# First row tile of weights and tokens loaded in row halves on two DMA queues, all its high parts on ScalarE, in a gated mix of attention and MLP

## Chip, cores and metric

The kernel runs on one core of one Trainium2 chip. The metric is the device time of one execution in microseconds. The kernel before takes 392.97 us (median of 3 runs, 392.96 to 393.01).

## The reference

For tokens x (2048 rows of 448), two branches are mixed by a gate g, one number per row:

```python
g = sigmoid((x * gate_w).sum(-1))          # 2048
qkv = x @ wqkv                             # 448 -> 3 * 448, 16 heads of 28
# each row attends to 8 rows: itself and those 2, 4, .. 14 before it
a = (softmax(q . k * scale) @ v) @ wo      # 448 -> 448
b = relu(x @ w1 + b1) ** 2 @ w2 + b2       # 448 -> 1792 -> 448
out = g * a + (1 - g) * b
```

All arrays are float32.

## The kernel before, in words

Each matmul operand is split into a high part (rounded to the matmul's reduced type, fp32r) and a low part (what is left of it), and a product is made of three matmuls: high by high, high by low and low by high. High parts are mostly made by ScalarE (an ACTIVATE that copies), low parts by VectorE (a subtraction, which needs the high part).

The contraction over 448 is cut into row tiles of 128, 128, 128 and 64. The tokens are taken in four chunks of 512 columns (x is transposed on the host). For each chunk q, k and v are made (function `qkv_first` for the first chunk, `qkv_two` for the others), stored to DRAM and read back by the attention, which GpSimd and VectorE work on while TensorE makes the MLP branch. The output projection by wo comes last. Most instructions of ScalarE, VectorE, GpSimd and of SP's DMA queue are ordered by a planner in the kernel (`Plan`): each job has a cost, its dependencies and a priority, and TensorE's own time is advanced by constants (`MM448`, `MM512`, `START` for the first real matmul, `FIRST` for the three row tiles of the first chunk). The planner decides the order in which instructions are built into each engine's queue; no time of it is waited for on the chip.

The start of the program is written out by hand (lines 801 to 843) and runs ahead of the planner:

- lines 806 and 807: WARM = 19 matmuls of zeros (128 by 128 against 256 columns) on TensorE;
- lines 809 to 813: the buffers `raws[0]` (first weight block, wq, with two columns for the gate: 450 columns) and `rx` (first chunk of tokens, 512 columns), each with four row tiles. ScalarE's queue loads row tile 0 of the tokens, 128 rows, in two halves of 256 columns;
- lines 814 to 821: SP's queue loads row tile 0 of the weights (128 rows, 225 KB), then row tiles 1 to 3 of weights and tokens in turn, and after these the weights of k and v;
- lines 830 to 839: the split. For row tile 0, ScalarE makes the weights' high part (`wqh`, line 831), VectorE the high part of the first half of the tokens' columns (line 836), VectorE the low part of the weights (`wql`, line 838) and of the first half (line 839); ScalarE then makes the second half's high part (line 834) and VectorE its low part. For the later row tiles ScalarE makes both high parts;
- `qkv_first`, line 429: q of the first chunk, for the row tiles 0 to 2 with 12 matmuls each, 36 in all. A matmul holds 128 tokens (a slice of x) as its stationary operand and streams 452 columns of weights (450 and a gap). For row tile 0 the order is: high by high for the first and second 128 tokens, then those two by the low weights, then the low tokens by the high weights, and the same for the third and fourth 128 tokens (which need the second half of the token columns).

After this come the 64-row tiles and k and v (line 341), and so on to the last projection (line 1154), the last mix (line 1037) and the last store. Near the end, ScalarE copies the attention outputs read back (tiles named ot) into SBUF and PSUM (lines 1110, 1115, 1120, 1121), VectorE subtracts (1122, 1124), and tiny ACTIVATEs (line 736, "touches") mark points of TensorE's order for the dependency tracking.

Of the kernel before, what the change touches and what calls it, by code (L numbers as in the profile page):

```python
# [9 lines left out]
AF = mybir.ActivationFunctionType  # L10
# [4 lines left out]
P = 128  # L15
# [7 lines left out]
CH = 512  # L23
NQ = D + 2
# [7 lines left out]
MM448, MM512 = 189.2, 216.0  # L32
PE_LAT = 175.0
LAT = 60.0
START = 4900.0
ORDER = (3, 0, 1, 2)
WARM = 19
FIRST = (2700.0, 2350.0, 2300.0)
PP_BUFS = 4
ST_BUFS = 3  # L40
BT_BUFS = 8
# [142 lines left out]
def gated_mix_kernel(ctx: ExitStack, tc: tile.TileContext, xT, wqkv, w1, w2, wo, b1, b2, out):  # L184
    nc = tc.nc

    def f32(ap):
        return ap.bitcast(F32)

    def woven(w):  # L190

        if w.shape[1] == NQ:
            return bass.AP(tensor=w.tensor, offset=w.offset, ap=[list(w.ap)[0], [1, NH], [D // 2, 2]])
        return w.rearrange("p (i n) -> p n i", i=2)

    def woven_out(pt, n):
        return (pt[:, :2 * NH] if n == NQ else pt[:, :n]).rearrange("p (n i) -> p n i", i=2)
# [85 lines left out]
    def x_tiles(c):  # L283
        if c % 2:
            x_place[0] = xpool.tile([P, 8 * CH + 16], F32R, tag="x", name=f"x{c}")
            return [x_slot(j, 0 if c == 1 else 16) for j in range(4)]
        return [xap.tile([P, 2, CH], F32R, tag=f"x{j}", name=f"x{c}_{j}") for j in range(4)]
# [11 lines left out]
    wqh = ap.tile([P, 3, NP + 2 * D], F32R, name="wqh")  # L299
    wql = ap.tile([P, 3, NP + 2 * D], F32R, name="wql")  # L300
# [119 lines left out]
    def qkv_first(x):  # L420
        four = range(4)
        q = accs(0, 0, four, "bbbb")
        for k in range(3):
            todo = [full(x, q[i], i, 0, (k,)) for i in four]
            for some in ((0, 1), (2, 3)) if k == 0 else (four,):
                for j in range(3):
                    for i in some:
                        acc, a, w, *_ = todo[i][j]
                        nc.tensor.matmul(woven_out(acc.pt, NQ), a, woven(w), start=k == j == 0, stop=False)  # L429
            plan.pe(FIRST[k])  # L430
        for acc in q:
# [373 lines left out]

    for _ in range(WARM):
        nc.tensor.matmul(warm[:, :2 * P].rearrange("p (i n) -> p i n", i=2), zero, zeros, start=True, stop=True)  # L807

    raws = [rawp.tile([P, 4, 512], F32, tag="raw", name="wqraw0")]
    rx = rawp.tile([P, 4, 512], F32, tag="raw", name="xraw0")  # L810
    halves = slice(0, 256), slice(256, CH)
    for cols in halves:
        nc.scalar.dma_start(rx[:, 0, cols], xT[0, :, 0, cols])
    for k in range(4):
        if k < 3:
            nc.sync.dma_start(raws[0][:, k, :NQ], wqkv[0, :, k])
        else:
            for b, rows in ((0, slice(0, 64)), (1, slice(64, P))):
                nc.sync.dma_start(raws[0][rows, k, :NQ], wqkv[b, rows, k])
        if k:  # L820
            nc.sync.dma_start(rx[:, k], xT[0, :, k])
# [7 lines left out]
    x = X(x_tiles(0))  # L829
    for k in range(3):  # L830
        nc.scalar.activation(wqh[:, k, :NQ], raws[0][:, k, :NQ], AF.Copy)
        for n, cols in enumerate(halves if k == 0 else (slice(0, CH),)):
            if k or n:
                nc.scalar.activation(x.h[k][:, cols], rx[:, k, cols], AF.Copy)
            else:
                nc.vector.tensor_copy(x.h[k][:, cols], rx[:, k, cols])
            if not n:
                nc.vector.tensor_sub(wql[:, k, :NQ], raws[0][:, k, :NQ], f32(wqh[:, k, :NQ]))
            nc.vector.tensor_sub(x.l[k][:, cols], rx[:, k, cols], f32(x.h[k][:, cols]))
    nc.scalar.activation(w7h[:, :NQ], raws[0][:, 3, :NQ], AF.Copy)  # L840
    nc.vector.tensor_sub(w7l[:, :NQ], raws[0][:, 3, :NQ], f32(w7h[:, :NQ]))
# [3 lines left out]

    plan.t, plan.wire = START, 15000.0
    plan.now = 9800.0
# [64 lines left out]
    for c in range(4):  # L912
        x = xs[c]
# [305 lines left out]
    rows = wo_d.rearrange("(i b) n -> i b n", b=14)  # L1219
# [31 lines left out]
    for g in range(2, 2 * NF):  # L1251
# [5 lines left out]
        if not f:  # L1257
            x, slots = X([nxt[j][0] for j in range(4)]), [nxt[j][1] for j in range(4)]
# [105 lines left out]
```

## Time and profile before

| what | value |
| --- | --- |
| median of 3 runs | 392.97 us (392.96 to 393.01) |
| the profiled execution's own time | 392.84 us |
| its span | 391.1 us |
| TensorE busy | 386.5 us (99%), 3829 matmuls |
| VectorE, ScalarE, GpSimd busy | 260.3, 205.4, 260.6 us |
| DMA | 73.75 MB, mean 189 GB/s |

The profiled execution's own time stands beside its span: the span runs from the first to the last recorded instruction, and 1.7 us of the time lie around it. In rows of the timeline the first number is the start in us from the span's start, the second the length of the row, which can merge several instructions (xN); in square brackets stands how long the engine was idle before it and what ended the idle time. PE is TensorE, PEld its weight loads, ACT ScalarE, DVE VectorE, POOL GpSimd, SP SyncE; ACTq and SPq are instructions that issue DMAs. In rows of a table by stretch the two first numbers are the stretch and its length, then come the busy times of PE, PEld, DVE, ACT and POOL with their instruction counts, then the granted clock of TensorE, the busy share of the DMA engines and GB/s.

### The profile page before, as it was taken

What the parts mean: (1) busy time and instruction counts of PE and PEld (TensorE: products, weight loads), DVE (VectorE), ACT (ScalarE), POOL (GpSimd) and SP (SyncE); (2) the same over time, 40 slices, a digit from 0 to 9 for tenths busy, and PEclk for the clock granted to TensorE, in tenths of its full rate; (3) what the DMA queues carried; (4) which work ended last, traced back from release to release, by engine and by line L of the source; (5) the groups of instructions that cost most, each with busy time, mean ns of one, the idle gap of its engine ahead of it and who ended that gap; (6) DMA issues with size and microseconds to landing.
All of it is one profiled execution on the core that took longest, in us unless ns stands there. A gap on an engine that the chain in (4) does not pass through costs nothing.

```text
span 391.1 us, 9273 instructions
## 1 busy us (share of the span) xinstructions
PE 386.5 (99%) x3829; PEld 385.3 (99%) x3829; DVE 260.3 (67%) x346; ACT 205.4 (53%) x501; POOL 260.6 (67%) x165
## 2 busy tenths in 40 slices
PE   9999999999999999999999999999999999999996
PEld 8999999999999999999999999999999999999995
DVE  4525523588585778778656989789666686668454
ACT  5857865362566566445555445345716343456740
POOL 0000003979999989959999887999998979661000
PEclk9999999999999999999999999999999999999999
DMA  7999999997174062644203779645635220226835
GB/s 240 399 356 318 373 369 355 377 340 267 49 253 151 1 219 80 220 167 164 90 2 137 244 209 271 218 112 141 217 106 166 84 96 2 88 64 164 141 106 189
DMA packets 64697, 73.75 MB, mean 189 GB/s; under 512 B 32336, under 2 KB 57488, under 8 KB 64272
## 3 DMA queue, kind: packets, MB, share of 16 engines
q1 hardware_dynamic: 64224, 72.79, 56.4%
q8 instruction: 30, 0.49, 0.5%
q10 hardware_dynamic: 432, 0.38, 0.3%
q14 instruction: 11, 0.09, 0.1%
HBM read 45.71 MB, written 28.25 MB: 189 GB/s over the span
## 4 chain that ended last, share of the span: by engine, by line
PE 99%; DVE 0%; DVEq 0%; issue 0%
PE b L341 33%; PE h L341 32%; PE qkv L341 23%; PE a L341 7%; PE qkv L429 2%; PE warm L807 1%; PE a L1154 1%; DVE bt_b L1037 0%; DVEq L1359 0%
## 5 line engine op out<-in xcount | busy, mean ns | idle before, releaser
L539 POOL TENSOR_TENSOR pp<-q,k 128x896 f32<-128x896 f32 x56 | 116.8, 2119 | 75.1 <-DMA k<-k_d 63.5
L341 PE MATMUL h<-x,w1h 64*128 64x512 f32 x672 | 122.0, 376 | 0.0
L551 POOL TENSOR_TENSOR pp<-lg,v 128x896 f32<-128x896 f32 x64 | 113.9, 1868 | 9.4 <-DVE o L561 5.0
L341 PE MATMUL qkv<-wqh,x 64*128 64x448 f32 (+1 forms) x528 | 83.2, 350 | 0.0
L341 PEld LDWEIGHTS h<-x,w1h 64*128 64x128 f32 x672 | 82.8, 186 | 0.0
L341 PE MATMUL h<-x,w1l 64*128 64x512 f32 x336 | 75.9, 376 | 0.0
L793 DVE TENSOR_TENSOR h<-h,h 128x512 fp32r<-128x512 f32 x56 | 38.7, 691 | 55.1 <-ACT h L792 54.9
L543 DVE TENSOR_REDUCE lg<-pp 128x32 f32<-128x896 f32 x64 | 66.9, 1076 | 12.5 <-POOL pp L539 12.5
L341 PE MATMUL b<-w2bh,h 64*128 64x448 f32 x448 | 69.5, 349 | 0.0
L341 PE MATMUL b<-w2ah,h 64*128 64x448 f32 x448 | 69.2, 349 | 0.0
L561 DVE TENSOR_REDUCE o<-pp 128x112 f32<-128x896 f32 x64 | 67.5, 1066 | 0.0
L341 PEld LDWEIGHTS qkv<-wqh,x 64*128 64x128 f32 x528 | 61.0, 186 | 0.0
L341 PE MATMUL qkv<-wql,x 64*128 64x448 f32 (+1 forms) x264 | 56.8, 350 | 0.0
L789 ACT ACTIVATE h<-h,b1z 128x512 f32<-128x512 f32 x56 | 36.7, 655 | 37.1 <-PE h L341 37.1
L341 PEld LDWEIGHTS b<-w2bh,h 64*128 64x128 f32 x448 | 53.2, 193 | 0.0
L341 PEld LDWEIGHTS b<-w2ah,h 64*128 64x128 f32 x448 | 53.1, 193 | 0.0
L341 PE MATMUL b<-w2bl,h 64*128 64x448 f32 x224 | 47.6, 349 | 0.0
L341 PE MATMUL b<-w2al,h 64*128 64x448 f32 x224 | 47.5, 349 | 0.0
L341 PEld LDWEIGHTS h<-x,w1l 64*128 64x128 f32 x336 | 44.0, 186 | 0.0
L791 ACT ACTIVATE h<-h 128x512 fp32r<-128x512 f32 x56 | 33.4, 597 | 1.6
L363 ACT ACTIVATE st<-qkv 128x448 f32<-128x448 f32 x48 | 24.3, 539 | 17.8 <-PE qkv L341 11.5
L341 PEld LDWEIGHTS qkv<-wql,x 64*128 64x128 f32 x264 | 33.2, 186 | 0.0
(108 smaller groups left out, 576.4 us busy)
## 6 DMA issues: line engine op xcount, KB each, us to landing
v<-v_d SPq DMA_DIRECT2D x8, 840.0 KB, 6.8
x_d<-x SPq DMA_DIRECT2D x12, 512.0 KB, 7.3
x<-x_d SPq DMA_DIRECT2D x12, 512.0 KB, 4.1
k<-k_d SPq DMA_DIRECT2D x7, 840.0 KB, 7.4
q_d<-st SPq DMA_DIRECT2D x8, 448.0 KB, 5.8
k_d<-st SPq DMA_DIRECT2D x8, 448.0 KB, 5.7
v_d<-st SPq DMA_DIRECT2D x8, 448.0 KB, 6.4
o_d<-o SPq DMA_DIRECT2D x16, 224.0 KB, 2.1
```

The lines of the kernel that those rows point to most:

```text
L341: nc.tensor.matmul(woven_out(acc.pt, acc.n), a[rows], woven(w[rows]), start=acc.todo == acc.all, stop=acc.todo == 1)
L363: nc.scalar.activation(st[0][:, :, t % 2].rearrange("p (i g) c -> p i g c", i=2), unwoven(pt[:, :D]).rearrange("p i (g c) -> p i g c", c=C ...
L429: nc.tensor.matmul(woven_out(acc.pt, NQ), a, woven(w), start=k == j == 0, stop=False)
L539: nc.gpsimd.tensor_mul(pr.rearrange("p (w c) -> p w c", w=W), q[:, s:s + 1].to_broadcast([P, W, C]), k[:, s:s + W])
L543: nc.vector.tensor_reduce(lgs[i][:, s], pr.rearrange("p (w h d) -> p w h d", w=W, h=HG), axis=AX.X, op=ALU.add)
L551: nc.gpsimd.tensor_mul(pr.rearrange("p (h d w) -> p w h d", h=HG, w=W), lgs[i][:, s][:, :, :, None].to_broadcast([P, W, HG, DH]), vs[i][:, ...
L561: nc.vector.tensor_reduce(o_t[par, s][:, g * C:(g + 1) * C], pr.rearrange("p (c w) -> p c w", w=W), axis=AX.X, op=ALU.add)
L789: a = add(ACT, 656.0, lambda pt=pt, r=r: nc.scalar.activation(pt, pt, AF.Relu, bias=b1t[:, f + r:f + r + 1]), ready, bias_job[0], prio=NEXT)
L791: b = add(ACT, 600.0, lambda pt=pt, hh=hh: nc.scalar.activation(hh, pt, AF.Square), a, prio=NEXT)
L793: low = add(DVE, 690.0, lambda pt=pt, hh=hh, hl=hl: nc.vector.tensor_sub(hl, pt, f32(hh)), a, prio=NEXT)
L807: nc.tensor.matmul(warm[:, :2 * P].rearrange("p (i n) -> p i n", i=2), zero, zeros, start=True, stop=True)
L1154: nc.tensor.matmul(woven_out(acc.pt, D), a, woven(w), start=False, stop=acc.todo == 1)
```

## The change

- The first row tile of the weights (450 columns) and of the tokens (512 columns) is loaded in two halves of 64 rows each: rows 64 to 127 by ScalarE's queue, rows 0 to 63 by SP's queue, weights ahead of tokens on both. The loop that loads the later row tiles skips row tile 0.
- For row tile 0 ScalarE makes the high parts of both column halves of the tokens; VectorE's conversion of the first half is gone, and the low part of the weights is now ahead of all low parts of the tokens, as it was.
- One warm-up matmul less (WARM 18).
- The planner's constants START (4900 to 4800) and FIRST[0] (2700 to 2600).

```diff
-START = 4900.0
+START = 4800.0
 ORDER = (3, 0, 1, 2)
-WARM = 19
-FIRST = (2700.0, 2350.0, 2300.0)
+WARM = 18
+FIRST = (2600.0, 2350.0, 2300.0)
@@
     halves = slice(0, 256), slice(256, CH)
-    for cols in halves:
-        nc.scalar.dma_start(rx[:, 0, cols], xT[0, :, 0, cols])
+    for e, rows in ((nc.scalar, slice(64, P)), (nc.sync, slice(0, 64))):
+        e.dma_start(raws[0][rows, 0, :NQ], wqkv[0, rows, 0])
+        e.dma_start(rx[rows, 0], xT[0, rows, 0])
     for k in range(4):
+        if k == 0:
+            continue
         if k < 3:
             nc.sync.dma_start(raws[0][:, k, :NQ], wqkv[0, :, k])
@@
     for k in range(3):
         nc.scalar.activation(wqh[:, k, :NQ], raws[0][:, k, :NQ], AF.Copy)
-        for n, cols in enumerate(halves if k == 0 else (slice(0, CH),)):
-            if k or n:
-                nc.scalar.activation(x.h[k][:, cols], rx[:, k, cols], AF.Copy)
-            else:
-                nc.vector.tensor_copy(x.h[k][:, cols], rx[:, k, cols])
-            if not n:
-                nc.vector.tensor_sub(wql[:, k, :NQ], raws[0][:, k, :NQ], f32(wqh[:, k, :NQ]))
+        nc.vector.tensor_sub(wql[:, k, :NQ], raws[0][:, k, :NQ], f32(wqh[:, k, :NQ]))
+        for cols in halves if k == 0 else (slice(0, CH),):
+            nc.scalar.activation(x.h[k][:, cols], rx[:, k, cols], AF.Copy)
             nc.vector.tensor_sub(x.l[k][:, cols], rx[:, k, cols], f32(x.h[k][:, cols]))
```

## The prediction

> **What bounds the kernel now.** I read the page first, then who waited for whom on TensorE over the whole run, then the chain of waits of the first 20 us.
>
> ```profile
> span 391.1 us, 9273 instructions
> PE 386.5 (99%) x3829; PEld 385.3 (99%) x3829; DVE 260.3 (67%) x346; ACT 205.4 (53%) x501; POOL 260.6 (67%) x165
> ...
> PE 99%; DVE 0%; DVEq 0%; issue 0%
> ```
>
> ```profile
> PE warm L807 <- PEq L1356: 0.8, 1, 0.8
> ```
>
> ```profile
> 0.79 4.39 PE warm L807 x19
> 5.18 7.10 PE qkv L429 x36
> 12.28 86.71 PE qkv L341 x911
> ```
>
> The chain that sets the end is TensorE from 0.79 us on, and its one listed wait over the whole run is the 0.8 us ahead of the first instruction. So the kernel is a start-up, then an unbroken stream of matmuls, then a tail. The change can save only between 0.79 us and the first real matmuls, and whatever it delays there moves the whole stream. So the first 9 us are read one instruction at a time.
>
> ```profile
> 0.74 0.90 ACTq L813 DMA_DIRECT2D xraw<-xT  x2
> ...
> 0.75 0.86 SPq L816 DMA_DIRECT2D wqraw<-wqkv  x2
> ...
> 1.67 1.28 ACT L831 ACT_TABLE_LOAD   x1 [1.67 <-PEq L1356]
> ...
> 4.22 0.58 ACT L831 ACTIVATE wqh<-wqraw 128x450 fp32r<-128x450 f32 x1 [1.27 <-DMA wqraw<-wqkv]
> 4.40 0.29 DVE L836 CAST x<-xraw 128x256 fp32r<-128x256 f32 x1 [3.54 <-DMA xraw<-xT]
> 4.84 0.63 DVE L838 TENSOR_TENSOR wql<-wqraw,wqh 128x450 fp32r<-128x450 f32 x1
> ...
> 4.97 0.69 PE L429 MATMUL qkv<-wqh,x 128*128 128x452 f32 x2
> 5.38 0.42 DVE L839 TENSOR_TENSOR x<-xraw,x 128x256 fp32r<-128x256 f32 x1
> 5.52 0.30 PEld L429 LDWEIGHTS qkv<-wql,x 128*128 128x128 f32 x2 [0.21 <-DVE wql L838]
> 5.52 0.65 PE L429 MATMUL qkv<-wql,x 128*128 128x452 f32 x2
> ...
> 5.55 0.42 ACT L834 ACTIVATE x<-xraw 128x256 fp32r<-128x256 f32 x1 [0.75 <-DMA xraw<-xT]
> ...
> 5.88 0.56 ACT L831 ACTIVATE wqh<-wqraw 128x450 fp32r<-128x450 f32 x1
> ...
> 6.01 0.93 PE L429 MATMUL qkv<-wqh,x 128*128 128x452 f32 x4
> 6.34 0.61 ACT L834 ACTIVATE x<-xraw 128x512 fp32r<-128x512 f32 x1
> ```
>
> What to see: the weights' first row tile lands at about 4.2, the first half of the tokens at 4.4, the second at 5.5. The first matmul follows the last warm-up directly at 4.97; a wait for wql then takes 0.21. ScalarE loads its function table from 1.67 to 2.95, while it would wait for the weights anyway: that 1.28 costs nothing today.
>
> **The change part by part.** Before and after differ on TensorE by one warm-up matmul only; all other matmuls keep their order. The constants START and FIRST are the planner's; they move a few instructions of other engines.
>
> *The loads.* The bytes are the same (225 KB of weights, 256 KB of tokens), but all token rows are now needed before the first matmul, not half of the columns. The second view is the DMA in 40 slices of 0.175 us from 0 to 7 us:
>
> ```profile
> GB/s 0 0 0 0 0 0 0 0 0 0 165 129 154 230 245 216 180 163 273 295 336 305 279 279 301 279 270 322 379 361 340 403 385 367 398 340 372 378 431 386
> ```
>
> The first bytes move at 1.75, 1.0 us after the issue at 0.75. Summed slice by slice, 230,400 bytes (the weight tile) have moved by 2.98, and 361,000 (with the half of the tokens that runs beside it) by 3.5; yet the weights were seen at 4.2, 0.7 after that. With the change the first 230,400 bytes are the two weight halves, so they land earlier than now. The half on SP's queue, call its landing S, lies between 3.28 (2.98 and 0.3, which I estimate from today's 0.7, taken as less than half of it since less traffic trails) and 4.2 (no better than the whole tile today). I take **3.45**: 230,400 bytes at the mean rate of 361,000 in the 2.15 us from 1.75 to 3.9 (4.2 less 0.3) need 1.37, so 1.75 + 1.37 + 0.3. The whole tokens are 131,000 bytes more than the 361,000 that are in by 4.4; at the 300 KB per us that the slices show there they land at about 4.4 + 0.44 = 4.85.
>
> In a sentence apart: the Trainium skill, "DMA: Bandwidth & Descriptors", section "Rules for kernel authors", says of two transfers to disjoint partition halves not to bother, since both use the same 16 engines, so it speaks against a gain from the two queues; by it S would be nearer 4.2. That the present loads on two queues land only 0.2 apart agrees with it.
>
> *ScalarE's table load.* This is the part on which my sum turns. The first ACTIVATE now needs two loads, one on each queue. In the built order of the changed kernel ScalarE's rows are
>
> ```
> 1 L813 DMACopy wqraw_149<-wqkv 64x450
> 2 L814 DMACopy xraw_150<-xT 64x512
> 3 L834 LoadActFuncSet [waits DMAHW1_49]
> 4 L834 Activation wqh<-wqraw_149 128x450 [waits DMAHW0_49]
> 5 L837 Activation x_0_172<-xraw_150 128x256 [waits DMAHW3_49,DMAHW2_49]
> ```
>
> where before the table load stood with no wait and one wait stood at the ACTIVATE. DMAHW1 is the weight half on SP's queue, DMAHW0 that on ScalarE's: the second wait became an instruction of its own, and the table load was put behind it. ScalarE runs in order, so the 1.28 no longer lies beside the loads but behind S. Queued behind it are all the high parts (wqh, then both halves of x), on these VectorE's low parts, and on both TensorE.
>
> *The sum*, with 0.05 for each handover (the wql subtraction ends at 4.84 + 0.63 = 5.47, its reader starts at 5.52; bounds 0 and 0.1): table load from 3.45 + 0.05 = 3.50 to 4.78; wqh from 4.83; the first half of x 0.47 later (as 5.88 to 6.34 now), at 5.30, done at 5.72 (0.42). The tokens have landed by then. First matmul at 5.77. wql: wqh ends 5.41, then 0.05 and 0.63, so 6.09; its reader stands 0.49 behind the first matmul at 6.26 (two matmuls after a wait take 0.49 now: 5.52 to 6.01), so no second wait. The fifth matmul follows 0.38 later at 6.64; its low part of x is done by 6.0 + 0.42. Today the fifth is at 6.01. **So +0.63**, with S and the handovers +0.4 to +1.4.
>
> *The warm-up matmul taken out* (about 0.22: 19 from 0.79 to 4.97) is worth nothing here: TensorE would wait from 4.76 to 5.77 instead of from 4.97. The CAST that VectorE loses (0.29) is replaced by 0.42 on ScalarE, already counted. SP issues one load more (about 0.43) ahead of the next weight tile; DMA is busy through, the total of bytes ahead of that tile (722,000) is the same, so I cost it at nothing. If that cover failed, the next tile would have over 1 us: its first user is the 13th matmul, now at about 7.5 and then at 8.2.
>
> *The other engines later.* Matmuls do not wait in the present run, and they now come 0.6 later against loads that do not. The built order moves a few rows: attention reductions on VectorE past subtractions, o_d stores and ot loads on SP, two bt loads ahead of the last ot loads, and the second copy of the last ot past a touch of woh. Only those last have a short way to the end:
>
> ```profile
> 374.53 0.83 ACT L1110 ACTIVATE o<-ot 128x768 fp32r<-128x768 f32 x1
> 377.62 1.09 ACT L1115 ACTIVATE a<-ot 128x384 f32<-128x384 f32 x2 [2.26 <-DVE bt_a L1037]
> 379.23 0.20 ACT L736 ACTIVATE woh<-woh 128x1 fp32r<-128x1 f32 x1 [0.52 <-PE a L341]
> ```
>
> ```profile
> 383.59 0.46 PE L1154 MATMUL a<-woh,o 128*128 128x448 f32 x1
> ```
>
> Two loads more ahead (about 1 us) go into 2.26 idle; the moved copy would end near 379.9, and after one subtraction its reader at 383.59 still has about 3 us. Cost nothing.
>
> **The sum against the run.** The profiled execution took 392.84 with its span of 391.1; the median of the three timed runs is 392.97. The start-up delay enters one to one: 392.97 + 0.63 = **393.60 us**, 0.16% more. A measurement of this kernel tells about 0.2% (0.79 us) from no change.
>
> **The rivals.**
>
> *A. The table load stays early (faster or equal).* If it runs at 1.7 after all, wqh begins when both weight halves are there, and the first half of x when the tokens land. At 4.85: 4.85 + 0.42 + 0.05 = 5.32, the fifth matmul 0.87 later at 6.19, so +0.18: 393.15. From 4.67 down this case is faster than now; at 4.3 the first matmul would follow the 18th warm-up at 4.76, and the change would gain the 0.21 of the warm-up and at most the 0.1 of the wql wait: 392.7. Against it stands the built order. For it, that nothing in the present trace has a wait ahead of a table load.
>
> *B. The table load costs more than its row when nothing hides it.* After the load's end at 2.95, ScalarE shows nothing until 4.22, put down to the DMA. Up to 1.27 of that could be a settling time which the row can't show. Then +0.63 + 1.27: up to 394.9. Nothing in the trace speaks for it, and ScalarE does start right when the weights are there.
> In a sentence apart: the Trainium skill, "ScalarE: Activation LUTs", section "What ACT_TABLE_LOAD costs", gives about 1283 ns for the load, as the trace does, and about 1380 ns of drain for a switch to another set; by it, as an estimate, the time would be near 395.0, while here load and drain would have ended at 4.33, after the ACTIVATE began at 4.22.
>
> *C. The clock of TensorE rises later.* Warm-ups of 256 columns take 0.22, later matmuls of 452 columns only 0.19:
>
> ```profile
> 9.06 1.69 PE L429 MATMUL qkv<-wqh,x 128*128 128x452 f32 x8
> 10.59 0.93 PE L429 MATMUL qkv<-wql,x 128*128 128x452 f32 x4
> ```
>
> ```profile
> 4.00:5.00 1.00, 1.00 (x7) 1.00 (x6) 0.46 (x2) 0.58 (x1) 0.00 (x0) 1.00 0.94 299
> ```
>
> (8 in 1.53.) The granted clock reads 1.00 in every window, so it doesn't show this. The pace doubled some 4.3 us after the first warm-up, within the first real matmuls. The idle 1.0 us now lies right there. If it made the doubling start over at 5.77, matmuls would run at half pace for some 4.3 us: +2.15, 395.75. It decides only if about a quarter of idle time in those 4.3 us undoes it.
> In a sentence apart: the Trainium skill, "TensorE: Matmul & The Clock Gate", section "Part 1: The HAM clock gate", says that a free-running window of about 3.4 us, busy, lifts the half clock; one window more would cost, as an estimate, 1.7 us, 395.3. Against a free-running phase stand three runs within 0.05 us.
>
> *D. The planner's reordered rows make a stall later on.* The spare times above (2.26, about 3) speak against it; its price is one subtraction of 0.6 or so: 394.2.
>
> **How the numbers follow.** Forecast 0.66, A 0.08, B 0.14, C 0.09, D 0.03. The predicted time is the forecast's, 393.6. The range runs from 393.3 (the forecast's lower end is 393.37) to 394.9, which takes in its upper end (394.4), D and B; left out are A and C, 17 in 100, and a little at its lower end. Slower by over 0.2% (over 393.76): B, C, D and about a third of the forecast (S over 3.6): 0.26 + 0.22 = 0.48. Faster by over 0.2% needs 0.79, and all the time from the first landing to the first matmul is 0.75: 0.01. Within: 0.51.
>
> **What would show it.** In the changed kernel's trace: ScalarE's table load begins at about 3.5 instead of 1.67, right behind a DMA, with wqh at 4.8, and TensorE idle 1.0 between warm-ups and first matmul near 5.8. If the table load still begins near 1.7, A holds. If wqh begins over 0.3 after the load's end though both weight halves are there, B. If more than two of the real matmuls are 0.38 apart, C. If the fifth matmul is at 6.6 and the end is more than 0.3 off +0.6, then something later moved, D or worse, and the sum is wrong.

## The result, and the profile after

| | before | after |
| --- | --- | --- |
| median of 5 runs | 392.97 us (392.96 to 393.51) | 396.79 us (396.30 to 397.57) |
| ratio after / before | | 1.0093 [1.0082, 1.0105] |
| the profiled execution's own time, and its span | 392.84, 391.1 | 397.57, 395.7 |
| idle time of TensorE ahead of the first real matmul | none | 1.98 us |
| first real matmul, fifth | 4.97, 6.01 | 6.94, 8.61 |
| the 36 matmuls of line 429, in the chain of waits | 7.10 us | 10.04 us |

The change makes the kernel 3.82 us (about 1%) slower, outside the predicted range of 393.3 to 394.9. The profiled execution of after is the slowest of its five, so its rows show 4.6 us of span where the median lost 3.8.

From the page of after, the span, the engines' busy time and the shares of the chain that ended last:

```profile
span 395.7 us, 9272 instructions
PE 389.2 (98%) x3828; PEld 387.4 (98%) x3828; DVE 262.5 (66%) x345; ACT 205.7 (52%) x502; POOL 260.6 (66%) x165
...
PE 97%; DMA 1%; SPq 0%; DVE 0%; ACT 0%; DVEq 0%; issue 0%; ACTq 0%
```

TensorE is busy 2.7 us longer with one matmul less. No work was added to it, so it ran slower somewhere. The waits of TensorE now have a second row:

```profile
PE qkv L429 <- ACT x L837: 2.0, 1, 2.0
PE warm L807 <- PEq L1355: 0.8, 1, 0.8
```

The chain of waits of after (start, length, what), with its first pieces and one from the end:

```profile
1.38 5.01 DMA xraw<-xT
...
6.47 0.42 ACT x L837
...
6.94 10.04 PE qkv L429 x36
...
388.38 3.62 PE a L1153 x18
```

And that last piece in before:

```profile
383.67 3.62 PE a L1154 x18
```

The whole loss lies in the first 17 us. The 36 matmuls end at 6.94 + 10.04 = 16.98, in before at 5.18 + 7.10 = 12.28: 4.70 later. The last projection begins 388.38 - 383.67 = 4.71 later. So nothing between moved. Of the 4.70, the first matmul is 1.97 late (6.94 instead of 4.97), and from it to the end of the 36 it is 10.04 instead of 12.28 - 4.97 = 7.31, which is 2.73 more.

In the chain, ahead of the first matmul stand the token half on SP's queue, which lands at 1.38 + 5.01 = 6.39, and its high part. The timeline of after, where before had its first rows:

```profile
0.74 0.56 ACTq L813 DMA_DIRECT2D wqraw<-wqkv  x1
0.75 0.58 SPq L813 DMA_DIRECT2D wqraw<-wqkv  x1
...
1.33 0.61 ACTq L814 DMA_DIRECT2D xraw<-xT  x1
1.38 0.83 SPq L814 DMA_DIRECT2D xraw<-xT  x1
...
3.92 1.28 ACT L834 ACT_TABLE_LOAD   x1 [3.92 <-DMA wqraw<-wqkv]
...
5.22 0.58 ACT L834 ACTIVATE wqh<-wqraw 128x450 fp32r<-128x450 f32 x1
...
6.47 0.72 ACT L837 ACTIVATE x<-xraw 128x256 fp32r<-128x256 f32 x2 [0.68 <-DMA xraw<-xT]
...
6.94 1.12 PE L429 MATMUL qkv<-wqh,x 128*128 128x452 f32 x2 [1.98 <-ACT x L837]
```

The table load did move behind the weights (3.92), and wqh starts right at its end. But ScalarE was then idle again for 0.68, for the tokens. The same view for TensorE alone shows the pace:

```profile
8.61 1.71 PE L429 MATMUL qkv<-wqh,x 128*128 128x452 f32 x4
10.12 0.96 PE L429 MATMUL qkv<-wql,x 128*128 128x452 f32 x2
10.87 2.30 PE L429 MATMUL qkv<-wqh,x 128*128 128x452 f32 x6
13.01 0.93 PE L429 MATMUL qkv<-wql,x 128*128 128x452 f32 x4
13.77 1.69 PE L429 MATMUL qkv<-wqh,x 128*128 128x452 f32 x8
```

From 8.61 to 10.12 four matmuls (0.38 each), from 13.01 to 13.77 four as well (0.19 each). In before the same group of four, at 6.01, ran at 0.19. The trace's record of the clock has it doubled at 12.87; in before at 5.21. In all, 15 real matmuls start 0.375 or more behind the real matmul before them, in before none.

Two theories came out of this. **Tokens and clock**: the tokens land late, which starts the stream late, and the idle time ahead of it keeps TensorE's clock at half pace (the prediction's rival C). **Table load**: what the prediction turned on, the 1.28 of the load behind the weights, delays the start and all else follows from that.

### The profile page after: what moved, and what is told of

It reads as the page before. It is cut to its first block, busy times and chain, and to the rows that moved or that the text cites. A ratio compares the mean times of both kernels' runs of the same rounds, so it can differ in the third digit from the quotient of the medians.

```text
span 395.7 us, 9272 instructions
## 1 busy us (share of the span) xinstructions
PE 389.2 (98%) x3828; PEld 387.4 (98%) x3828; DVE 262.5 (66%) x345; ACT 205.7 (52%) x502; POOL 260.6 (66%) x165
## 4 chain that ended last, share of the span: by engine, by line
PE 97%; DMA 1%; SPq 0%; DVE 0%; ACT 0%; DVEq 0%; issue 0%; ACTq 0%
PE b L341 32%; PE h L341 32%; PE qkv L341 22%; PE a L341 7%; PE qkv L429 3%; DMA xraw<-xT 1%; PE a L1153 1%; SPq L813 0%; DVE bt_b L1036 0%; ACT x L837 0%; DVEq L1358 0%; ACTq L837 0%
```

## The experiments

All kernels compute the whole reference. A kernel's ratio is formed from all runs beside those of the kernel before on the same chip (393.09 to 393.23 us there), so it can differ a little from the ratio of two medians. Where a landing time is given without a row, it is the last completion of that load in the trace.

### The change with 32 warm-ups, so that TensorE has little idle time

```diff
-WARM = 18
+WARM = 32
```

> The change with 32 warm-up matmuls instead of 18, so that TensorE is busy until about 6.4 us. Theory (late start plus late clock: the idle time between warm-ups and first real matmul makes the pace of the matmuls double only near 13 us instead of 5.2): first real matmul stays near 6.9, those after it 0.19 apart at once, 394.2 us (393.9 to 394.8), the rest of the loss being the late start. Rival (the slow first matmuls come from something else, such as their operands or the DMA traffic): they stay 0.38 apart and the time stays at 396.3 to 397.6.

Measured: 394.60 us (394.26 to 394.75), ratio 1.0035 [1.0021, 1.0050]. The 36 matmuls in its chain of waits:

```profile
6.90 7.14 PE qkv L429 x36
```

The tokens land as late as in after (6.35) and the first matmul is as late (6.90), but the 36 matmuls take 7.14 instead of 10.04. So about 396.79 - 394.60 = 2.2 us of the loss is TensorE's clock, and the rest, 394.60 - 393.13 = 1.5, the later start.

### The change with the table load ahead

A one-element ACTIVATE on spare columns of a buffer, ahead of the split, brings the load forward.

```diff
+    nc.scalar.activation(b1z[0:1, 14:15], none, AF.Copy)
```

> The change with a tiny ACTIVATE ahead of the waits, so that ScalarE's table load runs near 1.7 us as before. Theory (the tokens land last, near 6.4): wqh begins near 3.9, but the high part of the tokens, and with it the first matmul, stays where it was, 396.3 to 397.0 us. Rival (the table load behind the wait, the step on which the prediction turned, sets the start): first matmul 1.3 earlier, 394 to 395.5 us.

Measured: 396.72 us (396.16 to 397.54), ratio 1.0092 [1.0076, 1.0108]: no gain. The load begins at 1.98, and then, in its timeline:

```profile
4.03 0.58 ACT L835 ACTIVATE wqh<-wqraw 128x450 fp32r<-128x450 f32 x1 [0.56 <-DMA wqraw<-wqkv]
...
7.20 0.72 ACT L838 ACTIVATE x<-xraw 128x256 fp32r<-128x256 f32 x2 [2.60 <-DMA xraw<-xT]
```

wqh is 1.2 earlier than in after (4.03 for 5.22) and it is worth nothing, because the first matmul waits for the tokens, which landed at 7.12 in this execution. That the load ahead is what made them later than in after (6.39) is unlikely: in the last run below, which has it too, they landed at 6.26. The table load theory falls for this kernel. The table by stretches of 1 us (columns as before; the third number from the right is the granted clock) shows the clock fall again:

```profile
7.00:8.00 1.00, 0.33 (x2) 0.33 (x3) 0.35 (x2) 0.80 (x3) 0.00 (x0) 1.00 1.05 361
8.00:9.00 1.00, 1.00 (x6) 0.93 (x5) 0.98 (x4) 0.92 (x2) 0.00 (x0) 0.75 0.83 175
9.00:10.00 1.00, 1.00 (x4) 0.92 (x3) 0.90 (x3) 0.58 (x1) 0.00 (x0) 0.50 0.78 223
...
11.00:12.00 1.00, 1.00 (x5) 0.89 (x4) 0.94 (x2) 0.69 (x2) 0.00 (x0) 0.54 1.05 391
12.00:13.00 1.00, 1.00 (x7) 0.99 (x6) 0.82 (x2) 1.00 (x3) 0.00 (x0) 1.00 1.05 398
```

0.75 over the stretch from 8 means full to 8.5 and half after; 0.54 over that from 11 means half until 11.92. The record has the clock up at 5.10, down at 8.51, up at 11.92: steps of 3.41 us.

### Before with 10 warm-ups: idle time alone

```diff
-WARM = 19
+WARM = 10
```

> The kernel before with 10 warm-ups instead of 19, nothing else: about 2 us idle on TensorE from 3.0 to 4.9. Theory (idle time ahead of the first matmuls delays the doubling of the pace): the first matmul starts near 4.9 as before, but 10 to 20 matmuls are 0.38 apart, 394.5 to 396.5 us. Rival (idle time of this length does nothing to the clock): 392.9 to 393.2 us.

Measured: 394.69 us (394.12 to 395.63), ratio 1.0036 [1.0020, 1.0053]. In the timeline:

```profile
5.00 1.12 PE L429 MATMUL qkv<-wqh,x 128*128 128x452 f32 x2 [1.74 <-ACT wqh L831]
```

The loads are those of before and the first matmul is only 0.03 later, yet the kernel is 1.6 us slower (394.69 against 393.13): 7 real matmuls run at half pace (10 to 20 were expected) and the clock doubles at 7.94. Idle time ahead of the stream costs time even if the stream starts when it did.

### The first row tile in whole tiles

One load of the weights by SP's queue, one of the tokens by ScalarE's; all else as in the change.

```diff
-    for e, rows in ((nc.scalar, slice(64, P)), (nc.sync, slice(0, 64))):
-        e.dma_start(raws[0][rows, 0, :NQ], wqkv[0, rows, 0])
-        e.dma_start(rx[rows, 0], xT[0, rows, 0])
+    nc.scalar.dma_start(rx[:, 0], xT[0, :, 0])
+    nc.sync.dma_start(raws[0][:, 0, :NQ], wqkv[0, :, 0])
```

> The change without the halves: the weight tile whole on SP's queue, the token tile whole (128 rows, one load) on ScalarE's queue; high parts all on ScalarE and 18 warm-ups as in the change. The table load then stands without a wait. Theory (the halves are what makes the loads late): tokens land by 4.9, first matmul near 5.3, 393.1 to 393.6 us if the pace doubles in time. Rival (needing all tokens at once is what is late, halves or not): tokens at 6 or later, 395 us or more.

Measured: 393.90 us (393.63 to 397.37, ten runs), ratio 1.0034 [1.0013, 1.0054]. The issues and the first ACTIVATE:

```profile
0.74 0.41 ACTq L812 DMA_DIRECT2D xraw<-xT  x1
0.75 0.39 SPq L813 DMA_DIRECT2D wqraw<-wqkv  x1
...
5.06 0.58 ACT L833 ACTIVATE wqh<-wqraw 128x450 fp32r<-128x450 f32 x1 [2.59 <-DMA wqraw<-wqkv]
```

The first issue on each queue takes 0.39 to 0.41 here, with 128 rows, and 0.56 to 0.58 in after, with 64. Uncut, the tokens land at 5.21, and the first matmul follows at 6.00, 0.94 ahead of after. In seven of ten runs it is 2.7 to 3.2 us faster than after's median; the other three are 395.41, 395.66 and 397.37. With 1.03 of idle time ahead of the first matmul the clock may decide run by run; the whole tiles with 27 warm-ups, below, test that.

### Halves by tensor: both weight halves on SP's queue, both token halves on ScalarE's

```diff
+    for rows in (slice(0, 64), slice(64, P)):
+        nc.sync.dma_start(raws[0][rows, 0, :NQ], wqkv[0, rows, 0])
+        nc.scalar.dma_start(rx[rows, 0], xT[0, rows, 0])
```

> The change with both weight halves on SP's queue and both token halves on ScalarE's; the same four loads of 64 rows. Theory (a load of 64 rows is as slow to issue as one of 128 or slower, and the halves double their number): tokens again near 6.4 us, first matmul near 6.9, 395.5 to 397.5 us. Rival (the two queues taking turns at one tile is what is slow): tokens by 5.2, first matmul by 6.2 behind the table load, 394 to 395 us.

Measured: 397.29 us (397.10 to 399.18), ratio 1.0115 [1.0090, 1.0139]. Whichever half is second on its queue is late. Here the tokens land at 3.84 and 5.01 and the weights at 4.30 and 5.82, the table load follows the weights (5.89), and the first matmul is at 8.12, 1.18 later still than in after; 9 real matmuls ran at half pace.

### Only the weights in row halves, then the same with the table load ahead

The tokens come in two column halves on ScalarE's queue, as in before, behind its weight half.

> Half of the change: the weight tile in row halves on the two queues, the tokens as before in two column halves of 128 rows on ScalarE's queue, behind the weight half; the rest as in the change, so the table load still stands behind the wait. Theory (table load behind the wait sets the start as soon as the tokens don't): table load near 3.9, wqh 5.2, first matmul 6.1 to 6.2. If the tokens are late here too, first matmul at 0.47 behind them. 394 to 396.5 us, by the clock.

Measured: 395.94 us (394.38 to 396.11), ratio 1.0061 [1.0040, 1.0082]. The weights land at 3.75 and 4.39, the load begins at 4.46, wqh at 5.75, the first matmul at 6.69; 9 real matmuls at half pace.

> As weight_halves, with a tiny ACTIVATE ahead of the waits that brings the table load to near 1.7. Theory (the wait ahead of the table load costs its 1.28 when the tokens are early enough): wqh near 3.9, first matmul 0.5 to 1.3 earlier than in weight_halves, 393.0 to 394 us. Rival (tokens land after 5.6 here too): no gain.

Measured: 394.51 us (394.02 to 395.29), ratio 1.0035 [1.0023, 1.0047]. wqh now begins at 4.33, yet the first matmul is at 6.90: the first token half, which here stands behind a weight half, landed at 6.41 in this execution (5.70 in the one before, where the load hid it). The expected gain at the start did not come. In this execution all 36 matmuls ran at full pace (7.14 in the chain, 8.82 without the load ahead), though TensorE was idle for about as long (1.94, and 1.84 without); so the lower time is the clock's, and that the load ahead made the difference is not shown.

### Only the tokens in row halves

> The other half of the change: the weight tile whole on SP's queue, the tokens in row halves on the two queues, SP's behind the weights; the table load has no wait ahead of it. Theory (each load of 64 rows issued late pushes what stands behind it): tokens between those of the whole tiles (5.2) and of the change (6.4), near 5.6; first matmul near 6.1; 393.6 to 396 us, by the clock. Rival (row halves of the tokens are by themselves what is late): 6.4 as in the change.

Measured: 394.25 us (393.64 to 396.15), ratio 1.0038 [1.0019, 1.0057]. The weights are whole on SP's queue and land at 3.54, the table load is early again (1.33, since the first ACTIVATE waits for one load), the tokens land at 4.91 and 5.51, the first matmul is at 6.06. With only three loads of the first row tile issued instead of four, the later token half lands 0.9 ahead of after's.

### The change with column halves

Same queues, same order, same bytes, but each load has 128 rows and half the columns.

```diff
-    for e, rows in ((nc.scalar, slice(64, P)), (nc.sync, slice(0, 64))):
-        e.dma_start(raws[0][rows, 0, :NQ], wqkv[0, rows, 0])
-        e.dma_start(rx[rows, 0], xT[0, rows, 0])
+    for e, n in ((nc.scalar, 1), (nc.sync, 0)):
+        c = slice(225 * n, 225 * n + 225)
+        e.dma_start(raws[0][:, 0, c], wqkv[0, :, 0, c])
+        e.dma_start(rx[:, 0, halves[n]], xT[0, :, 0, halves[n]])
```

> The change with column halves in place of row halves: all 128 rows of 225 weight columns and 256 token columns on each queue; the same number of loads and bytes, on the same queues in the same order. Theory A (loads of 64 rows are slow to issue and slow to begin): issues near 0.42 each and tokens by 5.3, 0.9 earlier than in the change; first matmul near 6.1 behind the table load; 393.8 to 396 us by the clock. Theory B (the number of loads and of bytes ahead of the first matmul is what counts, whatever the rows): tokens at 6 or later, first matmul near 6.9, 396 to 397.5 us.

Measured: 395.36 us (393.37 to 395.78), ratio 1.0037 [1.0015, 1.0059]. The token half that its chain of waits shows:

```profile
1.19 4.17 DMA xraw<-xT
```

Tokens at 5.36 and 5.61 instead of 5.90 and 6.39, first matmul at 5.86 instead of 6.94. For all of the tokens that is 0.78 which hangs on the 64 rows, and 0.2 to 0.4 comes with four loads in place of two (5.61 for the 5.21 of whole tiles; in the runs with 27 warm-ups below 5.37 for 5.18). The first matmul gains more, 1.08, because a column half is enough to start it and a row half is not.

### Before, with the weight load cut in two on SP's queue, without and with the table load ahead

This measures the disputed cost by itself: the tokens and all the rest are as in before.

```diff
+            for rows in (slice(0, 64), slice(64, P)):
+                nc.sync.dma_start(raws[0][rows, 0, :NQ], wqkv[0, rows, 0])
```

> The kernel before with its first weight load cut into two loads of 64 rows, both on SP's queue; tokens, CAST and 19 warm-ups as before. The first ACTIVATE now needs two loads, so the table load stands behind a wait here too. Theory (the table load behind the wait costs its 1.28 whenever nothing else is later): table load at 4.2 to 4.6, wqh 1.3 later, first matmul near 6.1 to 6.6 in place of 4.97; 394 to 396.5 us by the clock. Rival (the table load is hidden behind something anyway): 393 to 393.5.

> As weights_split_sp, with a tiny ACTIVATE ahead of the waits that brings the table load to near 1.7. Theory: wqh as soon as both halves are there (4.2 to 4.6), first matmul 4.9 to 5.3, 393.0 to 393.6 us, so at least 1 us less than weights_split_sp; what is left against the kernel before is the price of the split load alone.

Measured: 396.90 us (396.74 to 397.81), ratio 1.0100 [1.0086, 1.0113], and with the load ahead 394.73 us (393.89 to 395.73), ratio 1.0046 [1.0030, 1.0062]. The timeline of the first, then of the second:

```profile
5.54 1.28 ACT L834 ACT_TABLE_LOAD   x1 [5.54 <-DMA wqraw<-wqkv]
...
7.47 0.84 PE L429 MATMUL qkv<-wqh,x 128*128 128x452 f32 x2 [2.62 <-ACT wqh L834]
```

```profile
1.63 1.28 ACT L832 ACT_TABLE_LOAD   x1 [1.63 <-PEq L1360]
...
5.97 0.65 PE L429 MATMUL qkv<-wqh,x 128*128 128x452 f32 x2 [0.93 <-ACT wqh L835]
```

Where the weights are last, the load behind them is paid in full: the first matmul is 1.5 later (7.47 for 5.97), 1.28 of it the load and 0.22 the weights, which landed at 5.47 and 5.25. With the clock it is 2.2 us of time. And one load cut into two on one queue lands at 5.47 and 5.25 instead of 4.20.

### Before with all high parts on ScalarE

Undoes the loads and keeps only the move of VectorE's conversion.

> The kernel before with only one part of the change: ScalarE makes the high part of the first token half in place of VectorE (0.42 behind wqh's 0.47 in place of 0.29 beside it). Theory: first matmul at 5.15 to 5.2 in place of 4.97, 0.0 to +0.25 us, same within what can be measured. Rival (this is a main part of the loss): +0.8 us or more.

Measured: 393.21 us (393.07 to 393.81, eleven runs), ratio 1.0005 [0.9996, 1.0014]. This part of the change costs nothing that can be measured in the time. The profiled execution, one of the slower (393.80), has the first matmul at 5.33, later than the 5.15 to 5.2 expected, and the clock doubled only at 6.94.

### Whole tiles, and column halves, with 27 warm-ups

> after_whole_tiles with 27 warm-ups, TensorE busy until about 5.9. Theory (its scatter of 393.6 to 397.4 us was the clock's): first matmul at 5.9 to 6.1, no matmul at half pace, 393.8 us (393.5 to 394.2) and no run above 394.6. Rival (the loads scatter): single runs near 396 again.

> column_halves with 27 warm-ups. Theory (row halves are slower than column halves by 0.8 to 1.0, the clock did the rest): first matmul at 5.9 to 6.2, no matmul at half pace, 393.8 us (393.4 to 394.2), 0.8 below after_warm32's 394.6. Rival (the rows make no difference): 394.4 to 394.8.

Measured: 394.17 us (393.77 to 394.37, ten runs), ratio 1.0021 [1.0011, 1.0030]; and 394.22 us (393.57 to 394.55, ten runs), ratio 1.0022 [1.0013, 1.0031]. With the idle time covered no run is above 394.6, where without it both kernels had runs above 395: their scatter was the clock's. The medians are no better than 394.2. In the profiled executions the clock doubled late among the warm-ups (6.58 and 5.88), and 27 of them then end after the data is there (first matmul at 6.64 and 6.31); with column halves a matmul also waits for the second row tile's tokens, which landed at 8.20 and stand in its chain of waits. Column halves were expected 0.8 below the change with 32 warm-ups and are 0.4 below it.

### The change with 32 warm-ups and the table load ahead

> The change with 32 warm-ups and the early table load, so both known prices taken out. Theory (with the tokens last, the table load costs nothing): as after_warm32, 394.6 us (394.2 to 395.0), first matmul 6.8 to 7.6. Rival (the table load does hold something): 0.4 less or better.

Measured: 394.72 us (394.43 to 394.79), ratio 1.0033 [1.0020, 1.0046], beside 394.60 without the load ahead. Its chain of waits, and the tokens' high part in its timeline:

```profile
0.78 6.62 PE warm L807 x32
7.40 6.87 PE qkv L429 x36
```

```profile
6.34 0.72 ACT L838 ACTIVATE x<-xraw 128x256 fp32r<-128x256 f32 x2 [1.88 <-DMA xraw<-xT]
```

In this execution the warm-ups set the start, since the clock doubled late (6.66), so its time alone does not settle what the load ahead is worth. The second row does: with the load ahead ScalarE still waits for the tokens, until 6.34, and without it they are begun at 6.43.

No version beat the kernel before.

## Why the prediction was wrong, by its own steps

In short: the sum put the landing of the tokens 1.54 us too early (4.85 for 6.39), and it left out that TensorE would run its first matmuls at half pace after the idle time.

**What bounds the kernel**: right. The loss is a start-up loss, and the last projection is late by the same 4.7 as the end of the first 36 matmuls.

**The loads**: this is the step that failed. It said that the whole tokens "land at about 4.4 + 0.44 = 4.85". They landed at 6.39. The share and the rate of the DMA engines in after, in 40 slices of 0.175 us to 7 us:

```profile
DMA  0000000000049498869201055888999899999997
GB/s 0 0 0 0 0 0 0 0 0 0 0 41 123 154 350 319 304 213 176 70 12 34 0 102 91 211 242 302 285 300 286 255 362 347 375 359 349 405 348 266
```

Two things were wrong in it. The first is the way from bytes to a landing. Added up, 492 KB, which is the first row tile of weights and tokens, had moved by 4.94. But by 6.39, when the last token half was in, 961 KB had moved: the engines had meanwhile carried the row tiles issued behind it. Bytes moved do not say whose bytes they are. The prediction's own rows said so: in before the second token half was seen at 5.5, when by the slices shown there 993 KB had moved, not 492. Taken from that row, the tokens could not have been put ahead of 5.5.

The second, from 5.5 to 6.39, is what the cutting added. The count itself is a microsecond late: 492 KB had moved by 3.93 in before and by 4.94 in after. The loads begin later (to 2.5 us SP's queue had moved 0.11 MB in before and nothing in after, although it issued its first load at 0.75 in both), SP's token half is issued 0.2 later than the second half in before (1.38 for 1.19), and the engines are nearly idle from 3.3 to 4.2. That it hangs on four loads of 64 rows is shown by whole tiles (5.21), column halves (5.61) and token halves alone (5.51), and again with 27 warm-ups (5.18 whole, 5.37 in column halves); with four loads of 64 rows, weights ahead of tokens, the four traced executions have 6.26 to 7.12. Why such loads travel so, and why the engines idle there, the runs don't settle.

S, the landing of SP's weight half, was 3.85 against 3.45, inside its bounds. "SP issues one load more", costed at nothing, came out right, though not for its reason ("DMA is busy through", while the engines were nearly idle for 0.9): no matmul waited for the next row tile, whose high parts start at 7.10 and 7.57, long before the 13th matmul at 11.63.

In a sentence apart: the Trainium skill, "DMA: Bandwidth & Descriptors", section "Rules for kernel authors", says of two transfers to disjoint partition halves not to bother and to use one transfer of 128 partitions; the runs bear it out and go further, since the halves were not equal but later (6.39 against 5.21 for the tokens).

**ScalarE's table load**: the mechanism was right and its weight was wrong. The load began at 3.92 behind a DMA as foreseen, and the wait it adds is real (1.28 of the 1.5 at the first matmul in the pair with the split weight load). But in the changed kernel it lies beside the wait for the tokens: ahead or not, 396.72 and 396.79, and with 32 warm-ups 394.72 and 394.60. So that the change came out slower, as forecast, is in part luck: the reason given for it costs nothing here.

**The sum**: with 6.39 for 4.85 it would have given the first half of x at 6.44, the first matmul at 6.91 and the fifth 0.87 later at 7.78, so +1.77 and 394.74. The change with the clock held by warm-ups has 394.60. So the sum fails in that one term, and in the clock.

**The warm-up taken out** was called worth nothing. It deepens the idle time by 0.2, and idle time has a price here, as 10 warm-ups in before show. Its own share wasn't measured.

**Rival C** had 0.09 and is what happened beside it. Its sign, more than two real matmuls 0.38 apart, is there 15 times, and its condition holds here: it "decides only if about a quarter of idle time undoes it". That its price, 2.15, is close to what the runs give (2.2) is luck: it was worked out as a doubling that starts over at the first real matmul and takes 4.3 us, but the clock doubled 5.9 after it in this execution, and goes by steps whose place differs from one execution to the next. TensorE's idle share in the two clock steps before 12.87 can be read off the table by stretches of 3.41 us of after, the length of a step where the clock changes more than once (listed at the end):

```profile
2.63:6.05 3.42, 2.33 (x11) 2.04 (x10) 0.22 (x1) 1.86 (x2) 0.00 (x0) 1.00 0.78 211
6.05:9.46 3.41, 2.52 (x7) 2.27 (x8) 2.92 (x6) 2.29 (x5) 0.00 (x0) 1.00 1.00 296
9.46:12.87 3.41, 3.41 (x11) 3.03 (x10) 2.13 (x5) 2.61 (x5) 0.00 (x0) 1.00 0.97 318
```

Busy 2.33 and 2.52 of 3.41, idle 32% and 26%: not lifted. Then 3.41 of 3.41, and the clock doubled. What weighed against C, that three runs of before lie within 0.05 us, was too little: in the later comparisons before ranges from 392.92 to 394.10. After itself spreads over 1.3 us, whole tiles over 3.7.

In a sentence apart: the Trainium skill, "TensorE: Matmul & The Clock Gate", section "Part 1: The HAM clock gate", gives a free-running window of about 3.4 us for this; the steps of 3.41 us, placed differently in every execution, agree.

**Rivals A, B, D**: refuted. The load did not stay early; wqh began at 5.22, 0.02 after the load's end (3.92 + 1.28), with no settling time; and later reorderings moved nothing.

**The range and the chances**: "slower" had 0.48, but the range stopped at 394.9 because C was left out of it. The first error could be seen in the rows at hand, by the second token half at 5.5. Whether C's condition holds could not: no row of before shows TensorE idle for long between matmuls, so with 1.0 us of idle time in the forecast it was a case for a larger chance and a wider range.

## What to carry to other kernels

When a load is to be timed from bytes and rates, check the count against a load that the trace shows landing: here 492 KB had moved by 3.93 in before, and the last of them was seen at 5.5. Cover a wait at the start of a kernel with warm-ups up to the first real matmul, because idle time there can cost twice, once as delay and again as half pace; too many of them delay the start themselves (the runs with 27). An ACTIVATE that needs a second DMA can put the wait ahead of ScalarE's table load; look at the built order, and give the load an instruction of its own that waits for nothing.

## What the runs showed of the hardware that was not expected

- The clock of TensorE changes on steps of 3.41 us (up 5.10, down 8.51, up 11.92 with the table load ahead; up 4.38, down 7.79, up 11.20 with the weight load split), and their place differs from execution to execution. Over one step, 2.14 to 2.52 us of TensorE busy did not raise it; 2.70 (halves by tensor, 2.27 to 5.68) and 2.94 (10 warm-ups, 4.53 to 7.94) did. At full clock, 0.84 (5.10 to 8.51) and 0.80 (4.38 to 7.79) lowered it, and 1.74 did not (token halves, 3.64 to 7.05). Between them the busy time of a step does not decide alone: 1.57 lowered it in weight halves (4.59 to 8.01), and 1.51 did not in the same with the table load ahead (5.00 to 8.41). What else does is open.
- A load of 64 rows takes longer to issue (0.56 and 0.58 us for the weight halves of after, 0.61 and 0.83 for the token halves) than one of 128 rows and the same bytes (0.39 to 0.46 in column halves), and two 64-row loads on one queue land later than one of 128 rows with the same data (5.25 to 5.47 against 4.20 to 4.38 in before, with 10 warm-ups and with all high parts on ScalarE).
